# The whole attention bias before the attention, the conversion of w_in later, and side work held to its half step

## The chip, the core and the metric

One Trainium2 chip, one of its cores. The metric is the device time of one execution in microseconds. The kernel before takes 996.6 us, the median of three runs (995.92 to 999.07).

## The reference, cut to what matters

Three stages follow each other. An attention with a bias that depends on position alone (4 batches, 8 heads, 576 positions, 64 dimensions per head), a two-layer MLP on its output (2304 tokens, 512 to 2048 to 512, a leaky step between), and a mixture of 8 experts with the best expert chosen per token.

```python
    scores = scale * np.matmul(q, k.transpose(0, 1, 3, 2))
    psi_rel = np.log1p(np.abs(rel))                       # rel = pos[i] - pos[j]
    psi_i = np.log1p(np.maximum(pos[:, None].astype(np.float32), 1.0))
    x = (psi_rel / psi_i)[..., None]
    h = np.maximum(x @ w1 + b1, 0.0)                      # 32 hidden units
    bias = h @ w2                                         # 8 heads
    scores = scores + bias.transpose(2, 0, 1)[None, :, :, :]
    attn = softmax(scores)                                # over j
    ...
    h = x @ w_in                                          # x: the attention's output
    g = np.maximum(0.01 * h, h)
    x1 = g @ w_out
    ...
    out[mask] = gate_w[mask, None] * (np.maximum(x1[mask] @ w1[e], 0.0) @ w2[e])
```

The bias is the same for all four batches. w_in and w_out come as 64-bit floats and are converted on the chip.

## The kernel before

The change touches the first of three phases, `phase1`: the bias, the attention, and the first matmul of the MLP (x @ w_in).

**The bias.** `bias_setup` prepares constants (`e.lw`, `e.bv`, `e.coef`; the four scalings of `e.coef` on line 219). The 576 rows of the bias are made in 36 blocks of 16 rows x 8 heads by `bias_units`. A block takes four relus of up to 576 columns (`bias_relu`, tiles `mk`; the table `RELU` says by letter which of the four run on VectorE, line 232, and which on ScalarE, line 230), then 8 or 12 matmuls into PSUM (`psb`, line 274), a scaled copy to SBUF (`bt`, 591 columns) and one write to DRAM (`e.bias_d`, line 290). Blocks 0 to 11 (`WIDE`) and 32 to 35 use a tile of two PSUM banks from the scores' pool `psS` and one copy on ScalarE (line 286); blocks 12 to 31 use the pool `psM` and two copies, ten of which are on VectorE (line 282) and thirty on ScalarE (line 280). Sixteen blocks are made before the attention starts; the other twenty are a queue of filler, one call of `next` for each.

**The attention.** A step is one batch, a pair of heads and 128 rows of queries (64 for the last piece of a batch, which then has one pass for both heads). There are 80 steps, 20 for each batch: steps 0 to 7 are the first half of the rows of batch 0, steps 8 to 19 its second half, and so on. A step loads its slice of the bias into a `prob` slot (`load_bias`, 4 slots, a fifth after step 7), computes scores on TensorE (`pss`, line 418), adds the bias and takes the maximum on VectorE (line 423), exponentiates on ScalarE (`exps`, line 431), normalises (lines 440 to 449; on GpSimd for batch 0), transposes on TensorE (`pst`, line 469, and `psx`, lines 487 and 491) with copies to `pth` and `ptt`, and at the end of a group of two or three steps multiplies by v (`values`, `psv`, line 505). `x_split` turns that into high and low parts `x`. Scores run two steps ahead of the transposes.

**w_in.** `w_in_split` converts one of 16 column groups: a load (`w_raw`, 512 KB, four buffers), three integer operations on VectorE that assemble 32-bit words (`convert_f64`, lines 101, 105, 109), a copy to the high part `wi` (on VectorE for groups 0 to 7, on ScalarE for 8 to 15) and a subtraction on VectorE for the low part. The loop over `spread` starts one group per step from the first steps on, so all 16 are converted by about step 19. `up_units` then makes x @ w_in for half a batch: 16 units of 12 matmuls (`psh`, line 530), each followed by a copy (`hst`) and a write.

**What sets the order.** The program's text is an intended order. `side(n, pos)` issues the loads, splits and conversions that are due in half step (n, pos). `Filler` holds generators and spends a quota of estimated nanoseconds on the oldest of them in each half step. A scheduler then sorts each engine's instructions by its own estimate of when their inputs are ready, so an instruction that is ready early moves ahead; `tc.issue_after(x)` keeps what is issued inside it behind instruction x. Each engine runs its list strictly in order. SP's list holds nearly all transfers.

## Time and profile before

| | |
|---|---|
| median of three runs | 996.6 us |
| the profiled execution | 993.58 us |
| its span, first to last instruction | 991.8 us |
| TensorE busy | 962.8 us (97%) |
| VectorE busy | 660.7 us (67%) |
| ScalarE busy | 562.9 us (57%) |
| GpSimd busy | 80.8 us (8%) |
| mean granted TensorE clock | 0.998 of full speed |

The profile is one execution recorded by the hardware. A window shows, for a stretch of time, how long each engine was busy; PE is TensorE's matmuls, PEld its weight loads, DVE VectorE, ACT ScalarE, POOL GpSimd. A group is all instructions of one line, engine, operation and tile. A timeline lists instructions by start; `x12` merges twelve in a row, and the time then runs from the first one's start to the last one's end. One matmul of 32-bit floats can be recorded as two. Matmuls overlap, and their ends are modelled. A wait names the engine that waited, what it was about to do, and what released it. Phase 1 ends near 530 us; the change does not touch what follows.

### The profile page before, as it was taken

The numbers are of one execution on the slowest core, as the hardware profiler recorded it, in microseconds if no ns is written. First come the engines' busy times: TensorE is split into PE (matmuls) and PEld (weight loads), VectorE is DVE, ScalarE is ACT, GpSimd is POOL, SyncE is SP. The second block draws the span as 40 slices with busy tenths as digits, with TensorE's granted clock in tenths as the row PEclk, the third lists the DMA queues.
The fourth block names the chain that finished last, engine by engine and source line by source line (L and its number), as shares of the span: only waits on it lengthen the run. The fifth ranks groups of instructions, "written<-read, shape, count | busy, mean of one in ns | idle before, by whom it ended". The sixth has DMA issues, their size and how long they took to land. (4 is left out here: it accounts for less than half of the span.)

```text
span 991.8 us, 19017 instructions
## 1 busy us (share of the span) xinstructions
PE 962.8 (97%) x6294; PEld 801.0 (81%) x6294; DVE 660.7 (67%) x1668; ACT 562.9 (57%) x1146; POOL 80.8 (8%) x85
## 2 busy tenths in 40 slices
PE   6999999999999999999999999999999999999997
PEld 2455878998899889998898888888878888888885
DVE  8999987456766898778667866579984355313313
ACT  7888787778865666656454333344462455424423
POOL 0123330000000000000000000001002111111111
PEclk9999999999999999999999999999999999999999
DMA  8988998546976788546186533436506257312510
GB/s 280 277 249 283 282 296 291 151 146 192 290 230 203 237 268 277 173 143 181 50 274 216 167 110 106 129 117 241 142 22 223 66 201 269 129 43 73 181 43 35
DMA packets 137600, 180.62 MB, mean 182 GB/s; under 512 B 19841, under 2 KB 89857, under 8 KB 137362
## 3 DMA queue, kind: packets, MB, share of 16 engines
q1 hardware_dynamic: 115554, 149.83, 48.8%
q10 hardware_dynamic: 18576, 18.97, 5.4%
q0 software_dynamic: 3360, 10.49, 3.1%
q8 instruction: 52, 0.85, 0.3%
q14 instruction: 58, 0.48, 0.2%
HBM read 196.65 MB, written 43.94 MB: 243 GB/s over the span
## 5 line engine op out<-in xcount | busy, mean ns | idle before, releaser
L530 PE MATMUL psh<-x,wi 128*128 128x256 f32 (+1 forms) x1536 | 225.2, 297 | 0.5 <-DVE hst L537 0.5
L530 PEld LDWEIGHTS psh<-x,wi 128*128 128x128 f32 x1536 | 211.0, 189 | 1.2 <-DVE hst L537 0.7
L431 ACT ACTIVATE prob<-prob,stat 128x576 f32<-128x576 f32 x144 | 111.3, 773 | 40.9 <-DVE stat L423 39.2
L423 DVE CUSTOM_DVE_ANT_0 prob<-pss,prob 128x576 f32<-128x576 f32 x144 | 108.0, 753 | 36.0 <-PE pss L418 32.1
L800 PE MATMUL psx<-woh,gh 128*128 128x512 f32 x288 | 113.1, 393 | 0.0
L800 PE MATMUL psx<-wol,gh 128*128 128x512 f32 x288 | 112.5, 391 | 0.0
L800 PE MATMUL psx<-woh,gl 128*128 128x512 f32 x288 | 112.2, 390 | 0.0
L72 ACT ACTIVATE gh<-g 128x512 fp32r<-128x512 f32 x72 | 45.2, 631 | 112.4 <-PE psx L800 94.5
L84 DVE TENSOR_TENSOR htl<-pt,hth 128x512 fp32r<-128x512 f32 x40 | 25.8, 686 | 121.3 <-ACT hth L72 121.3
L469 PE MATMUL pst<-ident,prob 128*128 128x128 f32 x576 | 87.9, 277 | 4.6 <-POOL prob L449 2.5
L469 PEld LDWEIGHTS pst<-ident,prob 128*128 128x128 f32 x576 | 65.8, 140 | 23.4 <-issue 12.7
L72 ACT ACTIVATE pth<-pst 128x512 f32<-128x512 f32 (+1 forms) x120 | 65.3, 549 | 28.3 <-PE pst L469 20.9
L418 PE MATMUL pss<-kt,qhi 128*128 128x288 f32 x256 | 80.2, 330 | 0.0
L1259 POOL DMA_INDIRECT xg<-x,gidx x22 | 23.4, 1063 | 607.9 <-DMA ws<-in_mw_dram 538.7
L418 PE MATMUL pss<-kt,qlo 128*128 128x288 f32 x256 | 72.3, 298 | 0.0
L505 PE MATMUL psv<-pth,vs 128*64 128x256 f32 (+1 forms) x512 | 70.2, 412 | 0.2 <-ACT bt L280 0.2
L817 DVE SCALAR_TENSOR_TENSOR junk<-x1s,en 128x512 bf16<-128x512 f32 x96 | 66.0, 688 | 2.0 <-DMA en<-en_d 0.9
L1290 PE MATMUL pu<-w1h,xh 128*128 128x512 f32 x160 | 64.9, 405 | 0.3 <-ACT xh L72 0.3
L1321 PE MATMUL pd<-w2h,hth 128*128 128x512 f32 x160 | 62.8, 393 | 0.7 <-ACT hth L72 0.7
L800 PEld LDWEIGHTS psx<-woh,gl 128*128 128x128 f32 x288 | 54.1, 188 | 11.1
L274 PE MATMUL psb<-mk,coef 128*32 128x79 f32 (+49 forms) x640 | 50.0, 405 | 13.4 <-DVE mk L232 8.8
L800 PEld LDWEIGHTS psx<-woh,gh 128*128 128x128 f32 x288 | 54.1, 188 | 10.9
(223 smaller groups left out, 1831.7 us busy)
## 6 DMA issues: line engine op xcount, KB each, us to landing
ws<-in_mw_dram SPq DMA_DIRECT2D x164, 512.0 KB
prob<-bias SPq DMA_DIRECT2D x64, 288.0 KB
g<-h SPq DMA_DIRECT2D x72, 256.0 KB
prob<-bias SPq DMA_DIRECT2D x64, 256.0 KB
bias<-bt SPq DMA_DIRECT2D x36, 295.5 KB
h<-hst ACTq DMA_DIRECT2D x64, 160.0 KB
w_raw<-in_w_in_dram SPq DMA_DIRECT2D x16, 512.0 KB
h<-hst ACTq DMA_DIRECT2D x64, 128.0 KB
```

Source lines behind the costliest of these rows:

```text
L72: nc.scalar.activation(out=out, in_=in_, func=AF.Copy)
L274: nc.tensor.matmul(ps[32 * q:32 * q + 32, :b - a], lhsT=e.coef.rearrange("p g h -> p (g h)"), rhs=x, start=True, stop=True, tile_position= ...
L418: nc.tensor.matmul(ps[:, jh, :288], lhsT=lhsT, rhs=kt[:, c0 + 288 * jh:][:, :288], start=(k == 0), stop=(k == len(ops) - 1),)
L423: nc.vector.tensor_tensor_reduce(out=prv, in0=ps[:, :, :288], in1=prv, scale=-0.125, scalar=3.0e38, op0=ALU.add, op1=ALU.min, accum_out=st ...
L431: nc.scalar.activation(out=pr[:, h], in_=pr[:, h], func=AF.Exp, bias=stat[:, 0, h:h + 1], scale=-1.0, accum_out=stat[:, 1, h:h + 1],)
L469: nc.tensor.transpose(ps[:, 128 * c:128 * c + 128], pr[:, h, 64 * h + 128 * c:][:, :128], e.ident)
L505: nc.tensor.matmul(ps[64 * h:64 * h + 64, :n], lhsT=vs[:, c, h], rhs=ph[:, h, c, :n] if c < 4 else pt[:, :n], start=(c == 0), stop=(c == 4 ...
L530: nc.tensor.matmul(ps[:, :n], lhsT=w[:, kc], rhs=x[:, kc, :n], start=(k == 0), stop=(k == 3 * KD - 1),)
L800: nc.tensor.matmul(ps, lhsT=a[:, c % 4], rhs=w[:, c], start=(k == 0), stop=(k == 3 * KF - 1))
L817: nc.vector.scalar_tensor_tensor(out=junk, in0=x1, scalar=1.0, in1=e.en[:, k], op0=ALU.mult, op1=ALU.mult, accum_out=e.dots[:, t, k:k + 1],)
L1290: nc.tensor.matmul(ps, lhsT=a[:, k], rhs=w[:, k, c], start=(i == 0), stop=(i == 3 * KD - 1))
L1321: nc.tensor.matmul(ps, lhsT=a[:, k], rhs=w[:, k], start=(k == 0 and j == 0), stop=(k == 7 and j == 2))
```

## The change

1. The whole bias is made before the attention: all 36 blocks use a pool of four two-bank PSUM tiles of its own (`psH`), closed afterwards; the pools of the attention (`psM`, `psS`, `psT`) are opened only then. Each block has one copy, on ScalarE. Of the 144 relus, ScalarE has 27 instead of 54. The buffers grow from 14 to 16 (`mk`) and from 5 to 7 (`bt`). The scalings of `e.coef` go from VectorE to ScalarE. The fifth `prob` slot exists from the start.
2. w_in is converted later: the first integer operation of group f stands in half step `WIN_AT[f]`, 11 to 56, every third half step, that is from step 5 to step 28; two raw buffers instead of four. A unit of `up_units` for group f is not issued before group f is converted (`e.wi_done`), and the filler may go on to a younger generator meanwhile. The quotas are set to match.
3. The side work of a half step (k and q splits, first words of a conversion) is issued behind the latest scores on VectorE (`e.behind`) and the latest exponential on ScalarE (`e.behind_act`). A second buffer for q.

```diff
-RELU = ("DDAD", "DADD", "DAAD", "ADDA")
-
-WIDE, RELU_BUFS, BIAS_BUFS = 12, 14, 5
+RELU = ("DDAD", "DDDA", "DADD", "DDDD")
+
+RELU_BUFS, BIAS_BUFS = 16, 7
...
-LEAD = 4
+LEAD = 2
+
+WIN_AT = (11, 14, 17, 20, 23, 26, 29, 32, 35, 38, 41, 44, 47, 50, 53, 56)
...
-    yield from convert_f64(nc, raw, t)
+    words = convert_f64(nc, raw, t)
+    with e.tc.issue_after(e.behind):
+        next(words)
+    yield
+    yield from words
...
+    e.wi_done = f + 1
...
-        nc.vector.tensor_scalar_mul(e.coef[ps, g], w2r[ps], aw8[ps])
+        nc.scalar.activation(out=e.coef[ps, g], in_=w2r[ps], func=AF.Copy, scale=aw8[ps])
...
+        ps = psh.tile([128, 2, 512], F32, tag="h", name="psb").rearrange("p a j -> p (a j)")
+        for a, b, d, falls in bias_pieces(m, o):
...
-        if both:
-            nc.scalar.activation(out=bt, in_=ps2[:, o:o + BC], func=AF.Copy, scale=scale)
+        e.behind_act = nc.scalar.activation(out=bt, in_=ps[:, o:o + BC], func=AF.Copy, scale=e.br[:, m:m + 1]).ins
...
     for f in range(KF):
+        while f >= e.wi_done:
+            yield None
...
     def side(n, pos):
-        for f, args in todo.pop((n, pos), ()):
-            f(*args)
+        with tc.issue_after(e.behind), tc.issue_after(e.behind_act):
+            for f, args in todo.pop((n, pos), ()):
+                f(*args)
...
-        n = 2 + f if f < KF // 2 else 3 + f
-        spread((2 * n - LEAD + 1) // 2, (1 - LEAD) % 2, lambda f=f: w_in_split(nc, e, f), 1)
+        k = WIN_AT[f] - LEAD
+        spread(k // 2, k % 2, lambda f=f: w_in_split(nc, e, f), 1)
...
-    bu = bias_units(nc, e, WIDE)
-    for k in range(16):
...
-        next(bu)
-    fl.add(bu)
+    with tc.tile_pool(name="psH", bufs=4, space=PSUM) as psh:
+        for k, _ in enumerate(bias_units(nc, e, psh)):
...
+            if k == 31:
+                keys(0)
+            if k == 32:
+                queries(groups[0])
+    early.__exit__(None, None, None)
+    e.late = ctx.enter_context(tc.tile_pool(name="late", bufs=1, side="left"))
+    e.wi.append(new_w_in(e.late))
+    at.free.append(PROBS)
+    e.psM = ctx.enter_context(tc.tile_pool(name="psM", bufs=2, side="right", space=PSUM))
+    e.psS, e.psT = (e.wide.enter_context(tc.tile_pool(name=n, bufs=2, space=PSUM)) for n in ("psS", "psT"))
...
-        quota = 40 * 800.0 / 6.5 if n < 8 else KF * 1600.0 / 8 if hf == 0 else (13 if b == 0 else 17) * 1280.0 / 12
+        if b == 0:
+            quota = 1067.0
+        elif n < 31:
+            quota = (6 * 1280.0 + KF * 1600.0) / 11
+        else:
+            quota = KF * 1600.0 / 8 if hf == 0 else 17 * 1280.0 / 12
...
-        if n == 7:
-            fl.drain()
-        else:
-            fl.run(quota / 2)
+        fl.run(quota / 2)
```

What this makes of the engines' lists. VectorE, the first blocks of the bias, before (mk are relus, kt and qlo the k and q splits, w_t the words of w_in):

```order
L232 TENSOR_SCALAR mk<-lw,v 128x528 x2
L232 TENSOR_SCALAR mk<-lw,v 128x512 x2
L101 TENSOR_SCALAR w_t<-w_raw 128x512
L232 TENSOR_SCALAR mk<-lw,v 128x512
L232 TENSOR_SCALAR mk<-lw,v 128x496
L105 SCALAR_TENSOR_TENSOR w_t<-w_raw,w_t 128x512
L232 TENSOR_SCALAR mk<-lw,v 128x496 x2
L232 TENSOR_SCALAR mk<-lw,v 128x480
L80 CAST kt<-kraw 64x576
```

and in the changed kernel the end of its bias stage, with the first scores (ISA prob) behind it:

```order
L239 TENSOR_SCALAR mk<-lw,v 128x528 x3
L239 TENSOR_SCALAR mk<-lw,v 128x544 x3
L82 CAST kt<-kraw 64x576
L82 CAST kt<-kraw 64x640
L86 TENSOR_TENSOR kt<-kraw,kt 64x576
L86 TENSOR_TENSOR kt<-kraw,kt 64x640
L239 TENSOR_SCALAR mk<-lw,v 128x560 x3
L86 TENSOR_TENSOR qlo<-qraw,qhi 128x512
L239 TENSOR_SCALAR mk<-lw,v 128x576 x4
L416 ISA prob,stat<-pss,prob 128x576
```

The relus stand together, without words of w_in between them, and no score comes before the last of them.

VectorE, early steps of the attention, before:

```order
L423 ISA stat 128x1
L440 TENSOR_SCALAR stat<-stat 128x2
L282 TENSOR_SCALAR bt<-psb,rr 128x336
L441 RECIPROCAL stat<-stat 128x2
L232 TENSOR_SCALAR mk<-lw,v 128x368
L423 ISA prob,stat<-pss,prob 128x576
L423 ISA stat 128x1
L105 SCALAR_TENSOR_TENSOR w_t<-w_raw,w_t 128x512
L232 TENSOR_SCALAR mk<-lw,v 128x368
```

and the end of the scores of step 3 with what follows in the changed kernel:

```order
L416 ISA prob,stat<-pss,prob 128x576
L416 ISA stat 128x1
L433 TENSOR_SCALAR stat<-stat 128x2
L434 RECIPROCAL stat<-stat 128x2
L86 TENSOR_TENSOR qlo<-qraw,qhi 128x512
L86 TENSOR_TENSOR kt<-kraw,kt 64x576
L86 TENSOR_TENSOR kt<-kraw,kt 64x640
L433 TENSOR_SCALAR stat<-stat 128x2
L434 RECIPROCAL stat<-stat 128x2
```

Relus, bias copies and words of w_in are gone from between the scores; the splits of k and q stay.

TensorE, two blocks of the bias in the middle of its making, before, with scores (pss) and transposes (pst) between the blocks:

```order
L274 MATMUL psb<-mk,coef 32x304 x3
L274 MATMUL psb<-mk,coef 32x287 x4
L469 MATMUL pst<-ident,prob 128x128 x4
L274 MATMUL psb<-mk,coef 32x320 x4
L274 MATMUL psb<-mk,coef 32x271 x4
L274 MATMUL psb<-mk,coef 32x336
L418 MATMUL pss<-kt,qhi 128x288
L418 MATMUL pss<-kt,qlo 128x288
```

and the last blocks of the bias in the changed kernel:

```order
L273 MATMUL psb<-mk,coef 32x481 x4
L273 MATMUL psb<-mk,coef 32x31 x4
L273 MATMUL psb<-mk,coef 32x79 x4
L273 MATMUL psb<-mk,coef 32x497 x4
L273 MATMUL psb<-mk,coef 32x15 x4
L411 MATMUL pss<-kt,qhi 128x288
L411 MATMUL pss<-kt,qlo 128x288
```

All bias matmuls stand ahead of the first scores now.

## Rows read from the trace of the kernel before

**Rows 1.** Windows: length, busy us (PE, PEld, DVE, ACT, POOL), clock, DMA share, GB/s.

```profile
0.00:30.00 30.00, 19.93 (x245) 8.92 (x245) 27.21 (x68) 22.46 (x37) 0.74 (x7) 1.00 0.87 278
30.00:89.70 59.70, 55.19 (x569) 29.79 (x571) 55.50 (x143) 54.03 (x122) 13.61 (x14) 1.00 0.88 265
89.70:147.80 58.10, 54.26 (x433) 45.48 (x426) 53.91 (x129) 44.70 (x112) 21.57 (x21) 1.00 0.92 291
147.80:217.50 69.70, 68.42 (x522) 61.63 (x521) 40.15 (x105) 53.24 (x120) 1.48 (x1) 1.00 0.61 192
```

**Rows 2.** Timeline, VectorE (start, duration): first scores of steps 0, 8, 20.

```profile
30.16 0.75 DVE L423 CUSTOM_DVE_ANT_0 prob<-pss,prob 128x576 f32<-128x576 f32 x1
...
89.74 0.76 DVE L423 CUSTOM_DVE_ANT_0 prob<-pss,prob 128x576 f32<-128x576 f32 x1
...
147.78 0.75 DVE L423 CUSTOM_DVE_ANT_0 prob<-pss,prob 128x576 f32<-128x576 f32 x1
```

**Rows 3.** VectorE groups to 147.8 us: count, busy us, mean ns, idle before.

```profile
L232 DVE TENSOR_SCALAR mk<-lw,v 128x576 f32<-128x576 f32 (+17 forms) x90 | 38.7, 470 | 0.2
...
L105 DVE SCALAR_TENSOR_TENSOR w_t<-w_raw,w_t 128x512 uint32<-128x512 uint32 x15 | 10.4, 696 | 0.0
...
L84 DVE TENSOR_TENSOR wi<-w_t,wi 128x512 fp32r<-128x512 f32 x14 | 9.7, 693 | 0.2
...
L101 DVE TENSOR_SCALAR w_t<-w_raw 128x512 uint32<-128x512 uint32 x15 | 6.9, 460 | 0.0
...
L282 DVE TENSOR_SCALAR bt<-psb,rr 128x208 f32<-128x208 f32 (+9 forms) x10 | 5.8, 578 | 0.8 <-PE psb L274 0.8
...
L219 DVE TENSOR_SCALAR coef<-wb,sg 32x8 f32<-32x8 f32 x4 | 0.9, 223 | 0.1
```

**Rows 4.** Timeline, VectorE: two runs of relus back to back.

```profile
8.30 2.19 DVE L232 TENSOR_SCALAR mk<-lw,v 128x576 f32<-128x576 f32 x5
...
25.34 1.42 DVE L232 TENSOR_SCALAR mk<-lw,v 128x400 f32<-128x400 f32 x4
```

**Rows 5.** Timeline, TensorE: one bias block; a dense stretch after 155 us.

```profile
30.16 1.20 PE L274 MATMUL psb<-mk,coef 128*32 128x224 f32 x16
...
158.77 0.38 PE L418 MATMUL pss<-kt,qhi 128*128 128x288 f32 x1
159.38 1.59 PE L530 MATMUL psh<-x,wi 128*128 128x256 f32 x12
160.81 0.60 PE L469 MATMUL pst<-ident,prob 128*128 128x128 f32 x4
161.16 0.38 PE L418 MATMUL pss<-kt,qhi 128*128 128x288 f32 x1
...
168.85 1.95 PE L505 MATMUL psv<-pth,vs 128*64 128x256 f32 x16
171.16 0.66 PE L469 MATMUL pst<-ident,prob 128*128 128x128 f32 x4
```

**Rows 6.** Waits between 147.8 and 500 us: total us, times, longest us.

```profile
DVE prob L423 <- PE pss L418: 31.9, 32, 2.0
```

**Rows 7.** Groups on ScalarE up to 147.8 us.

```profile
L230 ACT ACTIVATE mk<-lw,v 128x576 f32<-128x576 f32 (+17 forms) x54 | 34.1, 659 | 0.0
...
L286 ACT ACTIVATE bt<-psb,rr 128x591 f32<-128x591 f32 x16 | 12.1, 755 | 3.1 <-PE psb L274 2.2 <-ACT mk L230 0.8
```

**Rows 8.** Transfers, first 60 us: rate by 1.5 us slice, totals, bias writes.

```profile
GB/s 0 222 199 315 361 345 385 287 176 284 331 243 363 240 322 387 297 343 160 311 324 302 280 285 261 297 284 201 297 232 300 279 263 311 156 231 230 187 291 207
DMA packets 10441, 16.18 MB, mean 270 GB/s; under 512 B 1824, under 2 KB 5024, under 8 KB 10434
...
bias<-bt SPq DMA_DIRECT2D x23, 295.5 KB
```

**Rows 9.** Windows at start and end: TensorE and its granted clock.

```profile
0.00:6.00 6.00, 0.00 (x0) 0.00 (x0) 3.65 (x15) 1.56 (x2) 0.74 (x7) 1.00 0.61 184
...
988.00:990.00 2.00, 0.00 (x0) 0.00 (x0) 0.00 (x0) 0.00 (x0) 0.00 (x0) 0.59 0.32 120
```

More of the change, by code (lines that the diff above doesn't have):

```diff
@@ L231, in bias_relu @@
         else:
-            nc.vector.tensor_scalar(out=o, in0=x, scalar1=e.bv[:, k], scalar2=0.0, op0=ALU.add, op1=ALU.max)
+            e.behind = nc.vector.tensor_scalar(
+                out=o, in0=x, scalar1=e.bv[:, k], scalar2=0.0, op0=ALU.add, op1=ALU.max
+            ).ins
         out.append(mk)
@@ L248, in bias_pieces, with bias_units @@
     return out
-def bias_units(nc, e, wide):
+def bias_units(nc, e, psh):
     nm = S // 16
@@ L290, in bias_units @@
         nc.sync.dma_start(out=dst[:, :, :BC], in_=bt)
-        yield 1600
+        yield
 class Attention:
@@ L552, in add, with unit @@
         self.queue.append(units)
+    def unit(self):
+        for units in list(self.queue):
+            try:
+                ns = next(units)
+            except StopIteration:
+                self.queue.remove(units)
+                continue
+            if ns is not None:
+                return ns
+        return None
     def run(self, ns):
         self.debt += ns
-        while self.queue and self.debt > 0:
-            try:
-                self.debt -= next(self.queue[0]) or 0.0
-            except StopIteration:
-                self.queue.pop(0)
+        while self.debt > 0:
+            ns = self.unit()
+            if ns is None:
+                break
+            self.debt -= ns
         self.debt = min(self.debt, 0.0)
@@ L565, in drain, with finish @@
         self.debt = 0.0
+    def finish(self, units):
+        for _ in units:
+            assert _ is not None
+        if units in self.queue:
+            self.queue.remove(units)
 def phase1(ctx, tc, e):
@@ L621, in phase1, with queries, keys @@
     for f in range(KF):
[L622 to L623 removed]
+        k = WIN_AT[f] - LEAD
+        spread(k // 2, k % 2, lambda f=f: w_in_split(nc, e, f), 1)
     for c in range(KF):
         spread(34 + 2 * c, 0, lambda c=c: w_out_narrow(nc, e, c), 1)
+    e.wi_done = 0
     bias_setup(nc, e)
[L628 to L641 removed]
+    def queries(g):
+        with tc.issue_after(e.behind), tc.issue_after(e.behind_act):
+            at.q_hi(g)
+            at.q_lo(g)
+    def keys(p):
+        with tc.issue_after(e.behind):
+            at.kv_hi(0, p)
+            at.k_lo(0, p)
+    with tc.tile_pool(name="psH", bufs=4, space=PSUM) as psh:
+        for k, _ in enumerate(bias_units(nc, e, psh)):
+            if k == 4:
+                for p in range(2):
+                    at.q_load(groups[p])
+                    at.kv_load(0, p)
+                    at.v_load(0, p)
+            if k == 31:
[8 more added lines that the diff above has]
+    e.psS, e.psT = (e.wide.enter_context(tc.tile_pool(name=n, bufs=2, space=PSUM)) for n in ("psS", "psT"))
     for n in range(4):
@@ L649, in phase1 @@
     at.normalise(steps[0])
+    keys(1)
+    queries(groups[1])
     xs = prev = None
+    ups = []
     def values_out():
@@ L658, in values_out @@
         if pp == 0:
-            pool = e.xp if ph == 0 else e.late
-            xs = [pool.tile([128, KD, HALVES[ph][1]], F32R, tag=f"x{i}{ph}", name=f"x{i}", bufs=1) for i in range(2)]
+            pool, bufs = (e.xp, 2) if ph == 0 else (e.late, 1)
+            for units in ups[:-3 if ph == 0 else -1]:
+                fl.finish(units)
+            del ups[:-3 if ph == 0 else -1]
+            xs = [pool.tile([128, KD, HALVES[ph][1]], F32R, tag=f"x{i}{ph}", name=f"x{i}", bufs=bufs) for i in range(2)]
         at.x_split(prev, *xs)
         if pp == NP - 1:
-            fl.add(up_units(nc, e, pb, ph, *xs))
+            ups.append(up_units(nc, e, pb, ph, *xs))
+            fl.add(ups[-1])
         prev = None
@@ L703, in phase1 @@
             at.pop_group(g)
-            if n == 7:
-                early.__exit__(None, None, None)
-                e.late = ctx.enter_context(tc.tile_pool(name="late", bufs=1, side="left"))
-                e.wi.append(new_w_in(e.late))
-                at.free.append(PROBS)
             at.values(g)
@@ L1441, in program @@
         e.xp, e.cv = pool(up, "xp"), pool(up, "cv")
-        e.psM = pool(up, "psM", 2, side="right", space=PSUM)
         for n, b in (("const", 1), ("big", 1), ("small", 4), ("raw", 1), ("kvp", 1), ("ptp", 1)):
             setattr(e, n, pool(wide, n, b, side="right"))
-        e.psS, e.psT = (pool(wide, n, 2, space=PSUM) for n in ("psS", "psT"))
+        e.wide = wide
         tail = phase1(up, tc, e)
```

48 lines of the change are left out of this document (12 added, 36 removed).

## The prediction

> **What bounds the kernel now.** I read the windows first, cut where the attention's steps 0, 8 and 20 get their first scores (VectorE's operation on line 423 starts at 30.16, 89.74 and 147.78 us) and, at 217.5 us, step 31 [rows 1, 2]. Up to 147.8 us nothing is idle for long and nothing is full: between 30.0 and 89.7 us TensorE is busy 55.2 of 59.7 us, VectorE 55.5, ScalarE 54.0; between 89.7 and 147.8 us VectorE 53.9 and TensorE 54.3 of 58.1. From there on TensorE has no gap: 68.4 of 69.7 us, while VectorE falls to 40.2. So the kernel has two halves. Before step 20 VectorE, with ScalarE close behind, sets the pace, and TensorE is fed unevenly (its busy time there over-reads, since the ends of its matmuls are modelled). After step 20 TensorE alone counts, and whatever matmul work has not been done by then must still be done. The end therefore moves by two things only: how much earlier step 20 comes, and how much more TensorE work is then left.
>
> **The bias goes ahead of the attention.** The work on the bias is the same 36 blocks and 320 matmuls. The relus change engine: 27 move from ScalarE to VectorE (54 of 144 were on ScalarE, now 27), and the ten copies out of PSUM on VectorE go to ScalarE, where a block becomes one 591-wide copy. On VectorE 90 relus took 38.7 us [rows 3], 0.43 us each among other work; in runs five of about 570 columns took 2.19 us and four of 400 took 1.42 us [rows 4], which at the mean width of 440 is 0.374 us. They now stand in runs, so I price the 27 at 0.374: +10.1 us (0.43 would make it +11.6). The ten copies give back 5.8 us and the four coefficient scalings 0.9 us, which ScalarE now does before it has a relu to do [rows 3].
>
> **The conversion of w_in comes later.** In the order of instructions VectorE has, ahead of the scores of step 20, 15 first words, 29 second and third words and 14 low parts in the kernel before, and 9, 18 and 8 in the changed one. That is 6 x 0.46 + 11 x 0.696 + 6 x 0.693 = 14.6 us less [rows 3]. Six of the high parts leave ScalarE's stretch too, which is not the engine that sets the end here. The transfers of w_in move with the conversion: two raw buffers instead of four, issued on SP two half steps ahead. From the third column group on such a transfer waits on SP until VectorE has read the buffer two groups back, with the bias of a later step queued behind it; that bias is issued when a slot comes free, some three steps ahead of its scores, so I price this at 0. POOL keeps its 36 normalisations in their order.
>
> Removed in all: 5.8 + 0.9 + 14.6 = 21.3 us of recorded time. Records of neighbours on VectorE overlap (the 90 relus of 470 ns are 42.3 us, their busy time 38.7), so I take 0.915 of it: 19.5 us. Net -9.4 us of VectorE work before step 20.
>
> **What is added.** One hand-over: the scores of step 0 stand behind the last bias matmul on TensorE, so VectorE waits, after its last relu, for the last block (1.20 us) and the first four score matmuls (0.61 us) [rows 5]: +1.8 us. Until now VectorE had relus to fill such waits. In steps 0 to 7 it has nothing but attention and the k and q splits. A wait of VectorE for a score costs 1.0 us in the later stretch (31.9 us in 32) [rows 6]; with one in each step that would be +8 us, with none 0. VectorE already waits 4.2 us in steps 8 to 19 and that share is kept in my difference, and its order now has two steps of scores back to back with the q and k splits behind them, which cover the exponentials; I take 0 and keep 8 for the range. The waits on the transfer queue (16 relu buffers instead of 14, 7 block buffers instead of 5, a second q buffer) only loosen; I price them at 0.
>
> Step 20 then comes at 147.8 - 9.4 + 1.8 = 140.2 us, 7.6 us earlier.
>
> **What TensorE then still owes.** Ahead of the scores of step 20 stand 11 units of w_in matmuls now (132 matmuls of 256 columns) and 8 in the changed order. A unit is 1.43 us, from 159.38 to 160.81 us in the dense stretch [rows 5]: 3 x 1.43 = 4.3 us that have to be made up. The end moves by -7.6 + 4.3 = **-3.3 us**. The profiled execution took 993.58 us (span 991.8), 3.0 us under the median of 996.6; the same shift there gives **993.3 us**. Half a dozen VectorE operations per half step still follow in steps 20 to 30 (the conversions that came out of the earlier stretch), under TensorE: 40.2 + 14.6 us of 69.7.
>
> **Rivals.**
> *Larger gain.* VectorE's relus pack better than the 0.374 us, the hand-over hides behind the copies of the last blocks, and VectorE keeps full: -9.4 + 4.3 = -5.1, and with the 4.2 us of waits that steps 8 to 19 had before gone as well, -9.3. For it: nothing else is on VectorE in the bias stage. I give its middle, -7 us, 989.6.
>
> *No change: the bias stage has no single slowest engine.* TensorE needs 36 x 1.20 = 43.2 us [rows 5], ScalarE 27 x 0.63 + 36 x 0.755 = 44.2 [rows 7], VectorE 117 x 0.374 = 43.8. Three engines that need each other do not all run full: in the mixed stage they reached 0.93 of the time at best [rows 1]. 43.8 / 0.93 is 3.3 us more: end -3.3 + 3.3 = 0, 996.6. The same comes of the transfers: 36 blocks of 295.5 KB, q, k, v, two w_in columns and four steps of probabilities are 17.2 MB ahead of the last score of step 3, and the first 60 us moved 16.18 MB at 270 GB/s [rows 8], so 63 us for what VectorE would have done in about 60. Seven block buffers let the writes trail, hence at most the same 3 us. The Trainium skill (DMA: Bandwidth & Descriptors, Specifications) gives a limit of about 358 GB/s for a core's share of HBM; by it the 17.2 MB would take an estimated 48 us and never bind. The trace has slices of 385 and 387 GB/s above that and a mean well under it [rows 8]. Also here: a wait in half of the steps 0 to 7, +4.
>
> *Slower: TensorE is held by the late conversions.* Eight column groups are now converted in steps 20 to 30, where TensorE has no slack, and TensorE's order has the units that use them soon behind. A unit that reaches TensorE first waits for the third word and the low part, 0.70 + 0.69 = 1.39 us, with all scores queued behind it: 8 x 1.39 = 11.1 us, end +7.8, 1004.4. It outweighs the gain from 0.41 us per group on. Against it: VectorE is half idle there before, and no wait of these matmuls for a conversion shows now.
>
> *Slower, less likely: TensorE's clock falls.* Without units, a step keeps TensorE about 3.2 us (two sets of scores at 0.61, two of transposes at 0.35, half a set of values at 2.31) [rows 5] of some 4 us. The trace granted the full 2.4 GHz in the first 6 us, in which TensorE did nothing, and fell only after its last matmul at the very end, to 0.59 [rows 9]. At 1.2 GHz eight steps would take 51 us instead of some 32: +19 us.
> The Trainium skill (TensorE: Matmul & The Clock Gate, Part 1) says that the default state is throttled and that activity releases the throttle; by that rule the thin steps 0 to 7 could cost those 19 us. The idle first 6 us at full clock speak against it here, and no stretch of this trace tries a thin one for so long.
>
> **How the numbers follow.** About 0.3%, 3 us, is what a measurement of this kernel can tell from no change. Forecast (-6 to -1 us, middle -3.3): 0.44, of it 0.31 beyond 3 us. Larger gain: 0.13. No change, -1 to +3: 0.22. Late conversions hold TensorE: 0.18. Clock: 0.03. So faster 0.44, same 0.35, slower 0.21. The range goes from 988.0 (most of the larger gain) to 1001.5 (which leaves out the dearer half of the late conversions and the clock).
>
> **What would show it.** Right: first scores of step 0 at about 53.5 us (relus from some 5 us on, 43.8 us of them, 3 us of k and q splits, the hand-over of 1.8), of step 20 at about 140, and of step 8 at about 85 (steps 8 to 19 keep their 58.1 us less some 3 of conversions); TensorE without gaps from step 20 on, as now; 8 units done at step 20. Wrong in the first step of the sum: the last bias matmul later than 57 us, with VectorE idle for relu buffers or ScalarE's copies. Wrong in the second: steps 0 to 7 take over 34 us, with VectorE waiting for scores or exponentials. Wrong at the end: idle time of the unit matmuls behind VectorE's low parts between steps 20 and 31.

## The result

The changed kernel takes 1004.46 us, the median of five runs (1003.86 to 1006.94), against 996.6: the ratio is 1.0082, with a 95% interval of 1.0067 to 1.0097. It is about 8 us slower, where 3.3 us faster was forecast, and 3 us beyond the upper end of the range. The two profiled executions lie further apart, 1002.0 against 991.8 us of span, since that of before is one of its short ones.

The windows of the changed kernel, cut where the first scores of steps 0, 8, 20 and 31 and the last score of phase 1 start (columns as in [rows 1]), and the stretch behind phase 1's last score:

```profile
0.00:53.27 53.27, 43.31 (x647) 30.57 (x648) 47.50 (x131) 42.81 (x69) 0.74 (x7) 1.00 0.94 301
53.27:89.90 36.63, 29.87 (x185) 22.34 (x184) 31.54 (x74) 23.21 (x57) 15.42 (x16) 0.91 0.72 216
89.90:147.41 57.51, 53.56 (x370) 41.35 (x369) 54.43 (x126) 40.75 (x102) 25.02 (x20) 1.00 0.78 240
147.41:221.70 74.29, 72.99 (x523) 62.54 (x522) 47.77 (x124) 53.41 (x123) 0.00 (x0) 0.98 0.70 209
221.70:494.00 272.30, 271.38 (x2096) 242.23 (x2095) 205.11 (x556) 177.49 (x407) 0.00 (x0) 1.00 0.69 211
...
494.00:1002.00 508.00, 499.40 (x2483) 418.01 (x2481) 277.83 (x674) 211.90 (x360) 43.54 (x42) 1.00 0.42 137
```

and the last two of these of the kernel before, which [rows 1] leaves out:

```profile
217.50:487.00 269.50, 268.56 (x2082) 239.98 (x2082) 206.71 (x555) 177.31 (x403) 0.00 (x0) 1.00 0.68 210
487.00:991.80 504.80, 496.47 (x2460) 415.23 (x2458) 277.27 (x672) 211.12 (x358) 43.43 (x42) 1.00 0.43 138
```

| stretch | before, us | forecast | after | after - before |
|---|---|---|---|---|
| up to step 0 | 30.2 | 53.5 | 53.3 | +23.1 |
| steps 0 to 7 | 59.6 | 31.5 | 36.6 | -23.0 |
| steps 8 to 19 | 58.1 | 55 | 57.5 | -0.6 |
| steps 20 to 30 | 69.7 | gap-free | 74.3 | +4.6 |
| step 31 to the last score | 269.5 | | 272.3 | +2.8 |
| behind it | 504.8 | | 508.0 | +3.2 |

So three things went otherwise. Step 20 comes at 147.4 us, as before, and not at 140.2. Steps 20 to 30, which were to be free of gaps, then take 4.6 us more. And what TensorE owes costs 6.0 us (2.8 + 3.2), not 4.3.

VectorE ahead of step 20, in both kernels (groups: count, busy us, mean ns, idle before). Before:

```profile
L423 DVE CUSTOM_DVE_ANT_0 prob<-pss,prob 128x576 f32<-128x576 f32 x36 | 26.9, 751 | 1.8 <-issue 0.7 <-DMA prob<-bias 0.2 <-PE pss L418 0.2
L84 DVE TENSOR_TENSOR kt<-kraw,kt 64x576 fp32r<-64x576 f32 (+1 forms) x14 | 11.4, 817 | 0.4
...
L109 DVE SCALAR_TENSOR_TENSOR w_t<-w_raw,w_t 128x512 uint32<-128x512 uint32 x14 | 10.0, 716 | 0.0
...
L84 DVE TENSOR_TENSOR qlo<-qraw,qhi 128x512 fp32r<-128x512 f32 x9 | 7.1, 785 | 1.6 <-ACT qhi L72 1.6
...
L80 DVE CAST wi<-w_t 128x512 fp32r<-128x512 f32 x8 | 3.8, 477 | 0.0
L80 DVE CAST kt<-kraw 64x576 fp32r<-64x576 f32 (+1 forms) x8 | 3.8, 471 | 1.7 <-DMA kraw<-in_k_dram 1.4
...
L84 DVE TENSOR_TENSOR qtail<-qraw,qtail 128x128 fp32r<-128x128 f32 x4 | 1.2, 311 | 0.3 <-ACT qtail L72 0.3
```

After:

```profile
L239 DVE TENSOR_SCALAR mk<-lw,v 128x576 f32<-128x576 f32 (+17 forms) x117 | 42.2, 443 | 0.1
L416 DVE CUSTOM_DVE_ANT_0 prob<-pss,prob 128x576 f32<-128x576 f32 x36 | 26.4, 753 | 7.4 <-ACT bt L279 3.1 <-issue 2.5 <-PE pss L411 1.7
L86 DVE TENSOR_TENSOR kt<-kraw,kt 64x576 fp32r<-64x576 f32 (+1 forms) x14 | 13.2, 941 | 0.4
L107 DVE SCALAR_TENSOR_TENSOR w_t<-w_raw,w_t 128x512 uint32<-128x512 uint32 x9 | 8.0, 892 | 0.1
L111 DVE SCALAR_TENSOR_TENSOR w_t<-w_raw,w_t 128x512 uint32<-128x512 uint32 x9 | 7.1, 784 | 0.2
L86 DVE TENSOR_TENSOR qlo<-qraw,qhi 128x512 fp32r<-128x512 f32 x9 | 6.1, 676 | 0.0
L86 DVE TENSOR_TENSOR wi<-w_t,wi 128x512 fp32r<-128x512 f32 x8 | 5.8, 728 | 0.0
L82 DVE CAST kt<-kraw 64x576 fp32r<-64x576 f32 (+1 forms) x8 | 5.1, 632 | 0.1
L82 DVE CAST wi<-w_t 128x512 fp32r<-128x512 f32 x8 | 4.8, 594 | 0.0
L103 DVE TENSOR_SCALAR w_t<-w_raw 128x512 uint32<-128x512 uint32 x9 | 4.2, 465 | 0.0
...
L86 DVE TENSOR_TENSOR qtail<-qraw,qtail 128x128 fp32r<-128x128 f32 x4 | 2.6, 639 | 0.5 <-ACT qtail L74 0.5
```

Several of the same instructions on the same tiles got dearer: a copy of w_in's high part 0.594 instead of 0.477 us, the second words 0.892 instead of 0.696 [rows 3], the last part of q 0.639 instead of 0.311. Not all did: the other low parts of q went from 0.785 to 0.676 us, and the scores stayed at 0.75.

### The profile page after: what moved, and what is told of

Read it like the earlier page. It is cut to its first block, busy times and chain, and to the rows that moved or that the text cites. A ratio compares the mean times of both kernels' runs of the same rounds, so it can differ in the third digit from the quotient of the medians.

```text
span 1002.0 us, 19089 instructions
## 1 busy us (share of the span) xinstructions
PE 970.5 (97%) x6294; PEld 817.0 (82%) x6294; DVE 664.2 (66%) x1681; ACT 549.6 (55%) x1113; POOL 84.7 (8%) x85
## 5 line engine op out<-in xcount | busy, mean ns | idle before, releaser
L525 PE MATMUL psh<-x,wi 128*128 128x256 f32 (+1 forms) x1536 | 228.2, 298 | 0.5 <-DVE hst L532 0.4
L462 PE MATMUL pst<-ident,prob 128*128 128x128 f32 x576 | 90.4, 280 | 8.3 <-POOL prob L442 6.7
L498 PE MATMUL psv<-pth,vs 128*64 128x256 f32 (+1 forms) x512 | 76.4, 417 | 0.4 <-DVE hst L532 0.4
L834 PEld LDWEIGHTS psx<-woh,gl 128*128 128x128 f32 x288 | 54.1, 188 | 11.2
L1324 PE MATMUL pu<-w1h,xl 128*128 128x512 f32 x160 | 62.9, 394 | 0.0
```

Of the source, the lines that this page charges most:

```text
L462: nc.tensor.transpose(ps[:, 128 * c:128 * c + 128], pr[:, h, 64 * h + 128 * c:][:, :128], e.ident)
L498: nc.tensor.matmul(ps[64 * h:64 * h + 64, :n], lhsT=vs[:, c, h], rhs=ph[:, h, c, :n] if c < 4 else pt[:, :n], start=(c == 0), stop=(c == 4 ...
L525: nc.tensor.matmul(ps[:, :n], lhsT=w[:, kc], rhs=x[:, kc, :n], start=(k == 0), stop=(k == 3 * KD - 1),)
L834: nc.tensor.matmul(ps, lhsT=a[:, c % 4], rhs=w[:, c], start=(k == 0), stop=(k == 3 * KF - 1))
L1324: nc.tensor.matmul(ps, lhsT=a[:, k], rhs=w[:, k, c], start=(i == 0), stop=(i == 3 * KD - 1))
```

## The experiments

The letters in the expectations stand for theories. A: VectorE's side work (splits of k and q, conversion of w_in) is slowed by GpSimd's normalisations beside it. C: the late conversion costs. D: holding the side work behind the scores and exponentials costs. E: TensorE's lower clock costs. F: the emptied first steps cost. G: the owed units cost. Ratios are to the kernel before, run beside each.

### Without GpSimd's normalisations (a_nonorm, b_nonorm)

In each of the two kernels:

```diff
-            else:
-                nc.gpsimd.tensor_scalar(
-                    out=pr[:, h], in0=pr[:, h], scalar1=stat[:, 1, h:h + 1], scalar2=1.0, op0=ALU.mult, op1=ALU.mult
-                )
```

> The changed kernel with batch 0's 36 normalisations on GpSimd left out (its probabilities stay unnormalised, so GpSimd is idle during steps 0 to 19). Theory A (VectorE's splits and conversions are slowed by GpSimd working beside them): on VectorE the k low parts fall from a mean of 0.94 to about 0.79 us, the second words of w_in from 0.89 to 0.70, the high parts from 0.59 to 0.43; step 8 starts at about 85 instead of 89.9 us, step 20 at about 138 instead of 147.4, and the run is 7 to 9 us shorter than the changed kernel. Rival B (only TensorE's waits for GpSimd count, 4.2 us in steps 0 to 7 and 2.5 us in steps 8 to 19): VectorE's durations stay as they are and VectorE shows idle time instead; the run is at most 3 us shorter.

> The kernel before with batch 0's 36 normalisations on GpSimd left out, the counterpart of the same cut in the changed kernel, where VectorE's busy time ahead of step 20 fell from 133.5 to 122.8 us. Only the part up to the last score is read, since the time behind it depends on the values. Theory A (side work that stands together behind the scores meets GpSimd more than side work spread among relus): the fall is clearly less here, 136.6 to 130 to 133 us. Rival (GpSimd slows VectorE as much in both): it falls by 9 us or more, to 127 or less, and the slowing explains nothing of the difference.

Windows up to the first score of step 20, of before, after, after without the normalisations, and before without them:

```profile
0.00:147.78 147.78, 129.36 (x1236) 84.17 (x1237) 136.60 (x338) 121.18 (x268) 35.91 (x42) 1.00 0.90 278
```
```profile
0.00:147.41 147.41, 126.74 (x1199) 94.26 (x1199) 133.46 (x330) 106.77 (x226) 41.18 (x43) 0.98 0.82 256
```
```profile
0.00:143.94 143.94, 124.92 (x1199) 92.01 (x1199) 122.78 (x328) 105.56 (x225) 0.75 (x7) 0.99 0.83 262
```
```profile
0.00:144.95 144.95, 129.53 (x1238) 84.03 (x1238) 130.48 (x338) 120.38 (x265) 0.76 (x7) 1.00 0.90 280
```

VectorE's busy time falls by 10.7 us in the changed kernel (133.46 to 122.78) and by 6.1 in the kernel before (136.60 to 130.48). GpSimd slows VectorE in both, and by 4.6 us more in the changed kernel. The means in the changed kernel without normalisations:

```profile
L86 DVE TENSOR_TENSOR kt<-kraw,kt 64x576 fp32r<-64x576 f32 (+1 forms) x13 | 10.2, 784 | 0.4
L107 DVE SCALAR_TENSOR_TENSOR w_t<-w_raw,w_t 128x512 uint32<-128x512 uint32 x9 | 6.1, 681 | 0.0
...
L82 DVE CAST wi<-w_t 128x512 fp32r<-128x512 f32 x8 | 3.4, 422 | 0.0
```

Theory A stands for the durations. But step 20 comes only 3.5 us earlier, not 9: VectorE's idle time grows from 14.0 to 21.2 us. It was not the only one to set the pace, and A alone is not the loss. The kernel before gains nearly as much by the same cut, 2.8 us at step 20 (147.78 to 144.95), so what GpSimd costs more in the changed kernel is 0.7 us of step 20's time, though it is 4.6 of VectorE's. (The whole runs, 1018.22 and 1008.52 us, can't be compared: what follows phase 1 depends on the values.)

The Trainium skill (SBUF — State Buffer, Who interferes with whom) says that a VectorE instruction with two inputs in SBUF contends with a GpSimd instruction that reads SBUF, that casts and scalar operations can contend when they run in a mode that takes both port pairs, and that an instruction with at most one SBUF input outside those modes does not contend. The trace agrees: the slowed operations above have two SBUF inputs or are casts, and the scores, which have one input in PSUM, take 0.753 us with GpSimd and 0.755 without. It does not slow every such operation: the low parts of q take 0.676 us with GpSimd and 0.675 without.

### Normalisation partly on ScalarE (a_norm_act, b_norm_act)

```diff
-NORM = ("PDDD", "PAAA")
+NORM = ("ADDD", "PAAA")
```

> The changed kernel with the normalisation of the first head in batch 0 on ScalarE instead of GpSimd (20 of 36 operations, some 0.77 us each, where ScalarE is busy 107 of the first 147 us). Theory A: GpSimd's busy time ahead of step 20 halves, VectorE's falls by 4 to 6 us from 133.5, step 20 comes 2 to 4 us earlier than 147.4, and the run is 1.5 to 4 us shorter than the changed kernel. Rival (the chain from score to values sets the pace of these steps, and ScalarE's added work lengthens it): step 20 not earlier than 146, run within 1.5 us.

In the kernel before, for steps 8 to 19 alone:

```diff
-            w = NORM[h][st[0]]
+            w = NORM[h][st[0]] if st[:2] != (0, 1) or h else "A"
```

> The kernel before with the normalisation of the first head in steps 8 to 19 on ScalarE instead of GpSimd (12 operations; ScalarE is busy 44.6 of 58.0 us there). Theory A: VectorE's busy time in steps 8 to 19 falls by 1 to 2 us and the run is 0.5 to 2 us shorter than the kernel before. Rival: ScalarE delays the exponentials, and the run is within 1 us or longer.

The changed kernel: 1001.95 us, ratio 1.0071 (1.0056 to 1.0086), which overlaps the changed kernel's. VectorE's busy time ahead of step 20 falls by 4.4 us to 129.0, as A expected, and step 20 stays at 147.9, as the rival did. The kernel before: 994.64 us, ratio 1.0000 (0.9991 to 1.0009), no change, although VectorE's busy time in steps 8 to 19 falls by 3.3 us (53.9 to 50.6). Taking work from VectorE in these steps does not by itself bring the end forward.

### The bias ahead, and the late conversion, each alone (b_ahead36, b_ahead26, b_late)

```diff
-    for k in range(16):
+    for k in range(36):
```

> The kernel before with one number changed: all 36 bias blocks instead of 16 are made ahead of the attention, with its own pools, relu table, conversion of w_in and order of side work. Theory F (with the bias gone from the first steps TensorE runs thin after the hand-over, its clock falls, and VectorE's other work is left beside GpSimd): the granted clock shows stretches at half speed between the hand-over and step 20, 3 to 10 us of clock lost in all, and the run is 5 to 10 us longer than the kernel before. Rival (the place of the bias is neutral; the loss came from the late conversion and the held side work): within 2 us of the kernel before, clock 1.00.

The same with 26:

> The same with 26 blocks ahead and ten left as filler for steps 0 to 7. Theory F: TensorE keeps its clock while blocks are left, so at most one stretch at half speed and a run 0 to 4 us longer than the kernel before, clearly under that with 36. Rival: within 2 us of the kernel before, as the one with 36.

Part 2 alone in the kernel before (the table, `e.wi_done`, the filler that may pass a held generator, the quotas from step 8 on, two raw buffers):

```diff
-        n = 2 + f if f < KF // 2 else 3 + f
-        spread((2 * n - LEAD + 1) // 2, (1 - LEAD) % 2, lambda f=f: w_in_split(nc, e, f), 1)
+        k = WIN_AT[f] - LEAD
+        spread(k // 2, k % 2, lambda f=f: w_in_split(nc, e, f), 1)
```

> The kernel before with part 2 alone: w_in converted late by the table of the changed kernel, units held until their columns are converted, the quotas of the changed kernel from step 8 on; bias, relu table and side work as before. Theory F: the bias blocks still fill steps 0 to 7, so the clock stays 1.00 up to step 8; VectorE has 14.6 us less to do ahead of step 20, which comes 6 to 12 us earlier than 147.8; TensorE owes three units; the run is 2 to 6 us shorter than the kernel before. Rival (units that wait for late conversions leave TensorE empty around step 20): a stretch at half clock between 130 and 160 us and a run 0 to 6 us longer.

36 blocks ahead: 1000.7 us, ratio 1.0039 (1.0019 to 1.0060); 26 ahead: 999.32, 1.0029 (1.0013 to 1.0045). By the ratio 36 blocks cost about 4 us, between what F and its rival expected, and F's mechanism fails: with all 36 ahead the granted clock is 1.00 up to the last score. (With 26 it falls once; its mean in steps 8 to 19 is 0.97.) Step 20 comes at 155.5 and 154.1 us instead of 147.8, with the same relus and conversions as before: in this kernel, where ScalarE has 54 of the relus, a bias stage of its own costs 6 to 8 us at step 20. That the cost grows with the number of blocks is not shown, since the two intervals overlap.

Part 2 alone: 997.29 us, 1.0013 (1.0000 to 1.0026), no gain, and the clock stays 1.00. Step 20 comes 3.5 us earlier (144.3) and the last score 2.5 us later (489.5): the owed units take it back. With nothing held, the scheduler places some conversions earlier than the table says: 11 first words, 22 second and third words and 10 low parts stand ahead of step 20, not 9, 18 and 8. So 9.5 us of old work are removed there and not 14.6 (4 x 0.46 + 7 x 0.70 + 4 x 0.69); VectorE's busy time falls by 7.3 us (136.6 to 129.3), and that brought 3.5 at step 20.

### The conversion of before in the changed kernel (a_early)

```diff
-WIN_AT = (11, 14, 17, 20, 23, 26, 29, 32, 35, 38, 41, 44, 47, 50, 53, 56)
+WIN_AT = (5, 7, 9, 11, 13, 15, 17, 19, 23, 25, 27, 29, 31, 33, 35, 37)
...
-            quota = 1067.0
+            quota = 1067.0 if n < 8 else 13 * 1280.0 / 12
```

> The changed kernel with w_in converted in the half steps of the kernel before (first words in half steps 5 to 37) and the old quota for steps 8 to 19. Theory C (the late conversion is what costs: TensorE has no units left at 150 us, idles and owes three more): no gap of TensorE around 150 us, step 20 up to 10 us later than 147.4, but the whole 3 to 5 us shorter than the changed kernel (about 1000). Theory A (VectorE is the bound up to step 20 and its side work is slowed whenever it is done beside GpSimd): the 14.6 us of conversions come back ahead of step 20 and TensorE's three units (4.3 us) and its gap (2 us) go; the run is 5 us or more longer than the changed kernel.

1007.53 us, ratio 1.0101 (1.0059 to 1.0143); step 20 at 158.6 us. C falls: the old table gives nothing back. Step 20 comes 11.2 us later, and the three units that are then done cannot make up for it. The loss against the changed kernel that A expected, 5 us or more, is not shown either: by the ratios it is 2 us, and the intervals overlap.

### The clock (a_warm, a_warm2)

The granted clock fell twice in phase 1 of the changed kernel (windows, columns as above):

```profile
55.00:57.60 2.60, 0.56 (x4) 0.33 (x3) 2.53 (x8) 2.58 (x7) 0.76 (x1) 0.99 1.01 367
57.60:64.40 6.80, 6.51 (x26) 5.87 (x27) 6.04 (x12) 2.53 (x6) 2.73 (x4) 0.50 0.69 204
...
150.00:153.00 3.00, 1.79 (x10) 1.38 (x10) 2.87 (x10) 2.96 (x9) 0.00 (x0) 1.00 1.03 349
153.00:156.50 3.50, 3.50 (x12) 1.52 (x10) 3.37 (x9) 3.08 (x8) 0.00 (x0) 0.52 0.88 302
```

0.50 is 1.2 GHz. Ahead of the first fall TensorE was busy 0.56 of 2.6 us, ahead of the second 1.79 of 3.0. The first kernel adds transposes of the identity ahead of the real ones, the second fewer and only at the idle places:

```diff
         ps = e.psT.tile([128, 512], F32, tag="t", name="pst")
+        if h == 0:
+            for _ in range(e.warm):
+                nc.tensor.transpose(ps[:, :128], e.ident, e.ident)
...
+        e.warm = 16 if n < 8 else 12 if 18 <= n < 22 else 0
         at.transposes(st, 0)
```

> The changed kernel with extra transposes of the constant identity into the same PSUM tile ahead of the real ones: 16 for each of steps 0 to 7 and 12 for each of steps 18 to 21 (some 14 us of TensorE work in all, about 9 of it in steps 0 to 7, where TensorE is busy 62%). Theory E (the two stretches at half clock, 57.6 to 64.4 us and 153.1 to 156.5 us, are what costs): the granted clock stays 1.00, and the run is 2 to 5 us shorter. Rival (the first stretch lies under VectorE's work, which is busy without a gap from 55.6 to 63.8 us): the clock stays 1.00, steps 0 to 7 still take 36 us or more, and the run is within 2 us of the changed kernel or longer by part of the added work.

```diff
+        e.warm = {0: 16, 2: 12, 4: 8}.get(n, 0)
...
+                if h == 0 and jh == 0 and k == 0 and st == (1, 0, 1, 0):
+                    for _ in range(10):
+                        nc.tensor.transpose(ps[:, 0, 384:512], e.ident, e.ident)
```

> The changed kernel with extra transposes of the identity only where TensorE stood idle ahead of its two stretches at half clock: 16, 12 and 8 ahead of the transposes of steps 0, 2 and 4, and 10 ahead of the first scores of step 22 (46 in all, some 4.5 us of TensorE work in idle time). Theory E (the clock is about half of the loss): no stretch at half clock, 5.3 us of clock lost in the changed kernel's trace go to under 1, and the run is 3 to 5 us shorter than the changed kernel. Rival (the stretches lie under VectorE's work): the clock stays 1.00 but the run is within 1.5 us of the changed kernel.

The first: 1011.19 us, ratio 1.0151 (1.0118 to 1.0184), clock 1.00; the added work came out longer than the clock gave back. (TensorE is busy 82% of steps 0 to 7 by the window above, not the 62% of the expectation.) The second: 1002.05 us, 1.0061 (1.0041 to 1.0081), no fall of the clock up to the last score. Its steps:

```profile
53.41:90.49 37.08, 32.36 (x222) 23.77 (x222) 31.52 (x73) 23.38 (x57) 15.38 (x16) 1.00 0.69 217
...
147.63:220.45 72.82, 72.32 (x533) 62.92 (x532) 47.78 (x123) 53.38 (x123) 0.00 (x0) 1.00 0.70 213
```

Steps 0 to 7, 36 added transposes included, take as long at full clock (37.1 us) as with 6.8 us at half (36.6). VectorE is busy there from 55.6 to 63.8 us without a gap: the first fall lay under its work. Steps 20 to 30, where TensorE alone counts, give back 1.5 us (74.3 to 72.8), net of the ten transposes put in there (1.3 us busy). So the clock is about 2 of the 8 us by the traces, from the second fall. The ratios differ by 0.0021 too, but their intervals overlap.

### The hold (a_free, a_hold20, a_hold_dve, a_hold_act)

First nothing is held behind scores and exponentials, in any step:

```diff
-        with tc.issue_after(e.behind), tc.issue_after(e.behind_act):
+        if True:
...
-    with e.tc.issue_after(e.behind):
+    if True:
```

> The changed kernel with part 3 undone: the side work of a half step and the first words are not held behind the latest scores and exponentials. Theory D (holding them makes the splits of q and k late and puts them all into the time of GpSimd's normalisations): TensorE's wait of 2.2 us for the low part of q at 150 us goes, VectorE's slow splits become fewer, and the run is 3 to 5 us shorter. Rival: the scheduler puts them nearly where they are now, and the run is within 1.5 us of the changed kernel.

1005.08 us, ratio 1.0096 (1.0064 to 1.0127), which looks like the rival. But step 31 came at 215.2 us, 6.5 earlier than in the changed kernel, and the stretch from there to the last score took 276.1 us instead of 272.3 (in the profiled execution, 1001.08 us, which is the shortest of its four). So the hold was tried by stretches. Only from step 20 on:

```diff
-        with tc.issue_after(e.behind), tc.issue_after(e.behind_act):
+        hold = (e.behind, e.behind_act) if n >= 20 else (None, None)
+        with late_issue(tc, hold[0]), late_issue(tc, hold[1]):
...
-    with e.tc.issue_after(e.behind):
+    with late_issue(e.tc, e.behind if e.hold else None):
...
+        e.hold = n >= 20
```

> The changed kernel with its side work held behind scores and exponentials only from step 20 on; ahead of that the scheduler places it freely. Theory D in a new form (holding costs ahead of step 20, where VectorE is full, and pays behind it): step 31 at about 215 us as with nothing held, the stretch from step 31 to the last score about 272 us as in the changed kernel (276 with nothing held), and a run 3 to 5 us shorter than the changed kernel. Rival (the two stretches are coupled: what is won early is lost as soon as the owed units come due): the last score at 491 us or later, the run within 2 us of the one with nothing held.

995.27 us, ratio 0.9998 (0.9988 to 1.0009): the whole loss is gone, more than the 3 to 5 us that theory D had. Its windows (up to step 20 in all, then by stretch):

```profile
0.00:142.05 142.05, 124.54 (x1198) 90.63 (x1199) 128.84 (x334) 108.02 (x227) 34.50 (x43) 0.98 0.88 275
...
0.00:57.20 57.20, 46.73 (x647) 29.03 (x648) 54.33 (x145) 43.55 (x69) 0.74 (x7) 1.00 0.93 299
57.20:87.76 30.56, 26.40 (x162) 19.58 (x162) 28.12 (x72) 22.12 (x54) 11.13 (x13) 0.89 0.87 267
...
142.05:212.59 70.54, 69.86 (x525) 61.66 (x524) 45.84 (x118) 52.08 (x121) 0.12 (x1) 1.00 0.68 203
212.59:484.84 272.25, 271.35 (x2096) 242.18 (x2095) 205.05 (x556) 177.31 (x407) 0.00 (x0) 1.00 0.68 211
```

Step 20 comes 5.4 us earlier than in the changed kernel, and steps 20 to 30 take 70.5 instead of 74.3. What the hold does shows at the hand-over on VectorE (timeline: start, duration). With the hold:

```profile
48.36 1.80 DVE L239 TENSOR_SCALAR mk<-lw,v 128x576 f32<-128x576 f32 x4
53.27 0.76 DVE L416 CUSTOM_DVE_ANT_0 prob<-pss,prob 128x576 f32<-128x576 f32 x1 [3.11 <-ACT bt L279]
```

and without it:

```profile
52.28 1.80 DVE L242 TENSOR_SCALAR mk<-lw,v 128x576 f32<-128x576 f32 x4
54.00 0.68 DVE L114 SCALAR_TENSOR_TENSOR w_t<-w_raw,w_t 128x512 uint32<-128x512 uint32 x1
...
57.20 0.76 DVE L419 CUSTOM_DVE_ANT_0 prob<-pss,prob 128x576 f32<-128x576 f32 x1
```

Held behind a score, the side work can't fill the 3.1 us in which VectorE waits for that score; it is done later, behind scores, in steps in which GpSimd normalises. Without the hold 13 operations of w_in's conversion are done ahead of step 0, six of them in this gap and the others among the relus; with it none is. So VectorE is busy 54.3 us ahead of step 0 instead of 47.5, and GpSimd is idle there (0.74 us busy). VectorE's busy time ahead of step 20 is 128.8 us without the hold, with four operations more done by then, and 133.5 with it. The clock falls in steps 0 to 7 here too (0.89), and they still take 30.6 us instead of 36.6.

Then each of the two holds, behind the score on VectorE and behind the exponential on ScalarE, kept alone ahead of step 20:

```diff
-        hold = (e.behind, e.behind_act) if n >= 20 else (None, None)
+        hold = (e.behind, e.behind_act if n >= 20 else None)
...
-    with late_issue(e.tc, e.behind if e.hold else None):
+    with late_issue(e.tc, e.behind):
```

> The changed kernel with the side work held behind the latest scores on VectorE throughout, but behind the latest exponential on ScalarE only from step 20 on. Theory D1 (the hold on VectorE is what costs ahead of step 20: it sets the splits and conversions together, behind the scores and beside GpSimd): as the changed kernel, step 20 at 146 to 148 us, VectorE busy about 133 us ahead of it, the run 1002 to 1005 us. Rival D2 (the hold on ScalarE costs, since it delays the high parts of q that the low parts wait for): as with no hold ahead of step 20, step 20 at about 142 us, 995 to 997 us.

```diff
-        hold = (e.behind, e.behind_act) if n >= 20 else (None, None)
+        hold = (e.behind if n >= 20 else None, e.behind_act)
```

> The counterpart: held behind the latest exponential on ScalarE throughout, but on VectorE only from step 20 on. Theory D1: step 20 at about 142 us, VectorE busy about 129 us ahead of it, the run 995 to 997 us. Rival D2: step 20 at 146 to 148 us, 1002 to 1005 us.

VectorE's alone: 1002.59 us, ratio 1.0062 (1.0040 to 1.0084), step 20 at 148.0. ScalarE's alone: 997.83 us, 1.0019 (1.0006 to 1.0032), step 20 at 145.1. By the ratios D1 for the greater part, about 6 us, and D2 for about 2; the two add up to the whole. Step 20 itself does not follow so: D1 had it at 142 us without VectorE's hold, D2 at 146 to 148, and it came between them, 2.3 us earlier than in the changed kernel, while VectorE's busy time fell by 7.5 us (133.5 to 125.9). (That profile is of the longest of its twelve executions, 999.72 us.) Without ScalarE's hold it came no earlier, and without both 5.4.

### Fewer owed units (a_hold20_early)

```diff
-WIN_AT = (11, 14, 17, 20, 23, 26, 29, 32, 35, 38, 41, 44, 47, 50, 53, 56)
+WIN_AT = (7, 10, 13, 15, 18, 20, 23, 25, 28, 30, 33, 35, 38, 41, 44, 47)
...
-            quota = 1067.0
+            quota = 1280.0
```

> The kernel that holds only from step 20 on, with w_in converted somewhat earlier (first words in half steps 7 to 47 instead of 11 to 56) and a quota of 1280 instead of 1067 for batch 0. Theory G (the units that TensorE still owes at step 20 cost the end 6 us, and VectorE, idle 7.9 us in steps 8 to 19, can convert two more groups there): step 20 at 142 to 145 us with nine or ten units done, the run 1 to 3 us shorter than the one it is made from (992 to 994.5), a little under the kernel before. Rival (VectorE's added work in steps 8 to 19 comes out one for one): step 20 at 146 us or later and no gain, 995 to 998 us.

995.34 us, ratio 0.9993 (0.9981 to 1.0006), step 20 at 146.8. The rival: what is converted earlier comes out one for one. No version here beats the kernel before by more than its interval.

## Why the prediction was wrong, point by point

**The bias stage** was right: first scores at 53.27 us against 53.5, the 117 relus 42.2 us against 43.8, and no lack of a slowest engine. The hand-over cost 3.1 us instead of 1.8.

**VectorE's work ahead of step 20** is where the forecast broke. It was to fall by 9.4 us and fell by 3.1 (136.6 to 133.5). The relus are not the reason: added up one by one (117 of 443 ns against 90 of 470) they took 9.5 us more, where 10.1 stood. The error is in the other work. The conversions of w_in fell by 10.9 us of group time (40.8 to 29.9) and not by the 14.6 that the sum removes at the old means, and the splits of k and q, priced at no change, rose by 3.5 (23.5 to 27.0).

The step that failed: part 3, which holds the side work behind the scores, stands at nothing in the sum. "I take 0 and keep 8 for the range" was said of waits in steps 0 to 7 and not of what holding does to the work itself. In its place the runs showed that the hold ahead of step 20 costs the whole loss: without it (a_hold20) step 20 comes 5.4 us earlier, steps 20 to 30 take 3.8 us less, and the ratio goes from 1.0082 to 0.9998.

**How the hold costs** is shown in part. It leaves gaps empty that the work used to fill (the 3.1 us of the hand-over), and it makes the work dearer: without it the same means fall again (the copies of w_in's high part from 0.594 to 0.416 us, the low parts of k from 0.941 to 0.828). But that the dearer work is what delays step 20 is not shown. The sum let step 20 follow VectorE's work one for one, and the runs do not bear that out:

| run | VectorE busy ahead of step 20, us | step 20, us |
|---|---|---|
| before | 136.6 | 147.8 |
| b_nonorm | 130.5 | 145.0 |
| b_late | 129.3 | 144.3 |
| changed | 133.5 | 147.4 |
| a_norm_act | 129.0 | 147.9 |
| a_hold_act | 125.9 | 145.1 |
| a_nonorm | 122.8 | 143.9 |
| a_hold20 | 128.8 | 142.1 |

What else sets the pace of these steps under the hold stays open. The prediction's own sign of a failure there, steps 0 to 7 over 34 us, did come (36.6 us), but VectorE's idle time in them is 5.1 us against 4.2 before.

**Step 20** comes at 142.1 us with the hold gone, near the forecast of 140.2: VectorE is busy 128.8 us and idle 13.2 ahead of it, where the sum had 127.2 and 13.0. So the rest of that sum was about right.

**TensorE from step 20 on** was to have no more gaps than before. It had them at 150 us, and the longest, a wait for the low part of q, is gone without the hold (timeline of TensorE, with what ended its idle time):

```profile
150.43 0.37 PE L411 MATMUL pss<-kt,qhi 128*128 128x288 f32 x1 [0.52 <-DVE stat L416]
151.02 0.40 PE L411 MATMUL pss<-kt,qhi 128*128 128x288 f32 x1 [0.22 <-DVE stat L416]
151.98 0.40 PE L411 MATMUL pss<-kt,qlo 128*128 128x288 f32 x1 [0.56 <-DVE qlo L86]
```

The scores of step 22 wait for the low part of q, which VectorE makes at 151.26 us, behind four scores. In the 3 us from 150.0 TensorE is busy 1.8, and then its clock falls for 3.5 us. With either hold gone the stretch is 71.5 or 72.5 us, with both gone 70.5, against 74.3, and the clock stays 1.00 in it. Not all of this is placed: TensorE's idle time over the whole stretch is the same 1.3 us before and after (69.7 less 68.4, 74.3 less 73.0), the loss shows as busy time, and the clock is 1.5 us of it.

**The owed units** were mis-sized: 6.0 us (2.8 up to the last score, 3.2 behind it) where 3 x 1.43 = 4.3 stood. The count of three is right, but the units behind at step 31 are one of 256 columns and two of 320 (TensorE, matmuls up to step 31, by shape, before and after, and a unit of 320 columns in the timeline of the changed kernel):

```profile
L530 PE MATMUL psh<-x,wi 128*128 128x320 f32 x182 | 29.3, 309 | 0.0
L530 PE MATMUL psh<-x,wi 128*128 128x256 f32 x192 | 26.3, 284 | 0.0
```
```profile
L525 PE MATMUL psh<-x,wi 128*128 128x256 f32 x180 | 28.3, 296 | 0.1
L525 PE MATMUL psh<-x,wi 128*128 128x320 f32 x158 | 25.8, 310 | 0.0
```
```profile
160.13 2.01 PE L525 MATMUL psh<-x,wi 128*128 128x320 f32 x12
161.98 0.60 PE L462 MATMUL pst<-ident,prob 128*128 128x128 f32 x4
```

A unit of 320 columns took 1.85 us where it was followed at once (160.13 to 161.98 us), so 1.43 + 2 x 1.85 = 5.1 us were owed. The other 0.9 us stay open. The debt shows in other runs too: behind the last score the kernels with the old table of w_in take 503.3 to 505.0 us, those with the late one 507.1 to 508.5 (the two without normalisations left out), and a_hold20_early, whose table is earlier, 504.1.

**With both corrected** the forecast of the mechanism is seen in a_hold20: -5.7 us at step 20 (142.05 against 147.78) and about +6 owed give no change, and none is what it measured (ratio 0.9998).

**The rivals.** The slower one named 1004.4 us, and 1004.46 came, but not by its mechanism: it had TensorE wait 11.1 us for late conversions. Waits of the units' weight loads for conversions in steps 20 to 30:

```profile
PEld psh L525 <- DVE wi L86: 0.5, 2, 0.2
PEld psh L525 <- ACT wi L74: 0.2, 1, 0.2
```

0.7 us in all. The agreement of the number is chance. The clock, given 0.03, did fall, though for 10.3 us and not for all of steps 0 to 7, and cost about 2 us and not 19. (Its rows give 3.1 us of TensorE work a step, not 3.2: 49 us for eight steps and not 51.) The Trainium skill (TensorE: Matmul & The Clock Gate, Part 1) has the clock follow activity; both falls here come after stretches with idle time, which agrees, but where the first fell VectorE had the lead and the steps took no longer. The range ended at 1001.5 because the one part of the change that mattered was not in it.

## What to carry to other kernels

A rule on order (issue this behind that) is a change of its own: price it by the gaps that the held work used to fill, and by what runs beside it where it now stands. Work that is taken from one engine moves the end only until the next one is late: here 10.7 us less on VectorE moved step 20 by 3.5. A number that comes true is no proof of the mechanism that gave it; look at the wait that it named.
